# Idle products of the identity with itself ahead of tensor-engine parts in an attention and two-layer feed-forward kernel, with new seeds for its planner

## The chip, the cores and the metric

The kernel runs on one core of one Trainium2 chip. The metric is device time in microseconds (us), the median of several runs. The profile is one further execution, taken by the hardware profiler. Engines: PE is the tensor engine (matrix products, with weight loads beside them as PEld), DVE the vector engine, ACT the scalar engine, POOL the general one, SP the one that only issues transfers (DMAs). PSUM is the memory into which PE writes, SBUF the other on-chip memory.

## The reference, cut to what matters

Windowed attention over chunks of 32 queries (16 keys to the left, 8 to the right and 8 memory keys), then a gated layer (3072 tokens, 512 to 1536 to 512), then a second layer with softmax gating and normalization (512 to 1024 to 512).

```python
scores = scale * np.matmul(q_c, k_full.transpose(0, 1, 3, 2))
a = np.exp(scores - np.max(scores, axis=-1, keepdims=True))
a = a / (np.sum(a, axis=-1, keepdims=True) + 1e-09)
out[:, :, c_start:c_end] = np.matmul(a, v_full)
...
x = (1.0 / (1.0 + np.exp(-(x @ w_gate))) * (x @ w_val)) @ w_out
h = x @ w_in
solu = h * sm
ln = (solu - mu) / np.sqrt(var + 1e-06) * g_ln
return ln @ w_out2
```

## The kernel before, in words

The 3072 tokens are 24 tiles of 128, and 6 blocks of four tiles. Of each tile, attention is a chain of parts that change engines: raw keys `rk` and queries `rq` are loaded (SP, line 472), PE turns them (`d_k`, `d_q`, through `d_turn`, line 456: four transposes against `ident`), ACT and POOL copy them from PSUM to `kT` and `qT`, PE makes the score products (`d_scores`, through `two_banks`, line 515), DVE takes maximum and difference, ACT the exponential, DVE the sums, PE turns the result (`d_p`), ACT copies it to `pT`, PE multiplies with the values `vw` (`d_pv`, line 515), DVE normalizes into the tile `s` (line 597), PE turns it (`d_x`), and ACT and DVE split the turned rows into `xh` and `xl` (lines 610 and 614). The value tiles `vw` are loaded in many small transfers (lines 563 to 570) and completed from a small copy `mv` (line 583).

The weights arrive as raw 64-bit numbers in pieces of 512 KB (line 418). Each piece passes ACT (line 214), three DVE operations (lines 219, 220, 223), ACT (line 279) and POOL (line 230) before PE can use it as `wa`. Two pieces (gate and value) make one of 12 column groups m. `up(j, m, gv)` (line 629) is 12 products of 128x512 for block j into one PSUM buffer `u`; line 635 (ACT) and line 640 (DVE) read it. `down` (line 721), `prod` (line 774) and `out_mm` (line 866) are the later layers.

In PSUM the turned tiles and the `up` results share buffers: tag `u0` (two buffers) holds `d_k`, `d_x` and the memory keys, and `up` with gv 0; tag `u1` (two buffers) holds `d_q`, `d_p`, and `up` with gv 1. A part on PE waits until the buffer that it takes has been read out.

The order of all this is made by `Plan.order`: a list scheduler that knows a fixed duration of each part, its dependencies and its buffers, and takes of the parts that can start the one with the earliest due time. `SHIFTS` is a list of seeds and widths by which all due times are moved at random before it starts. What comes out is one order of instructions for each engine; the engines then run it in that order, each part when its inputs and buffers are there. Planned times are used for nothing else before.

Of the kernel before, what the change touches and what calls it, by code (L numbers as in the profile page):

```python
# [22 lines left out]
class Plan:  # L23
# [5 lines left out]

    HOP, WAIT, ISSUE, DGE, START, LAND, AHEAD, LANES = 0.2, 0.1, 0.48, 0.45, 0.75, 1.95, 40.0, 8  # L30

    SHIFTS = [(2011, 4), (2036, 2), (2116, 1), (2137, 0.5)]

    def __init__(self, caps):
        self.caps, self.tasks = caps, {}
# [98 lines left out]
def encoder_kernel(  # L134
# [313 lines left out]
        make_identity(nc, ident)  # L448


    def d_turn(tag, src):
        rows = src.shape[0]
        ps = pu.tile([128, 512], F32, tag=tag, name="tr")
        pv = ps[:, 0:KM * rows].rearrange("p (k r) -> p k r", k=KM)
        for kk in range(KM):
            nc.tensor.transpose(pv[:, kk, :], src[:, 2 * kk:2 * kk + 2, :], ident[0:rows, 0:rows])  # L456
        return pv
# [48 lines left out]

    def two_banks(lhsT, rhs):
        ps = pa.tile([128, 2, 512], F32, tag="a", name="ps")
        ps = ps[:, :, 0:KM * 64].rearrange("p x (k w) -> p x k w", k=KM)
        for kk in range(KM):  # L510
            for c in range(4):
                o = slice(CH * c, CH * c + CH)
                for x in range(2):
                    r = slice(D * x, D * x + D)
                    nc.tensor.matmul(ps[o, x, kk, :], lhsT=lhsT[r, kk, o], rhs=rhs[r, kk, c, :], start=True, stop=True)  # L515
        return ps
# [102 lines left out]

    def up(j, m, gv, w):  # L620
        u = pu.tile([128, 512], F32, tag=f"u{gv}", name="u")
        u = U[j, m, gv, w] = u[:, 0:w[1] - w[0]]
        xh, xl = X[j]
        n = 0
        for kk in range(KM):
            wh = wa[m][:, gv, 0, kk * 128:(kk + 1) * 128]
            wl = wa[m][:, gv, 1, kk * 128:(kk + 1) * 128]
            for a, c in ((wh, xh), (wh, xl), (wl, xh)):
                nc.tensor.matmul(u, lhsT=a, rhs=c[:, kk, w[0]:w[1]], start=(n == 0), stop=(n == 3 * KM - 1))  # L629
                n += 1  # L630
# [254 lines left out]
    ))  # L885
    add = plan.add
    ACT, DVE, POOL, PE, SP = "act", "dve", "pool", "pe", "sp"
    FIRST, RATE, LEAD, SLACK, EARLY, LATER = 30.0, 1.12, 30.0, 3.0, 140.0, 235.0

    ALONE = "c2", "nt", "gcol", "mhalf", "ident", "zero", "pb"  # L890

    def one(nm, t, eng, dur, fn, deps=(), **kw):
        add((nm, t), eng, dur, lambda: fn(t), deps=[d if isinstance(d, tuple) or d in ALONE else (d, t) for d in deps],
            prev=(nm, t - 1), **kw)
# [17 lines left out]
    for t in range(NTILE):  # L912
        n, u = divmod(t, 2)
        b, i = divmod(t, TB)
        early = t < 2
        one("rk", t, SP, 0.1, lambda t: d_load("rk", t), acq=[("rk", t)], dma=[1.456])
        one("dk", t, PE, 0.9 if early else 0.5, d_k, ["ident", "rk"], acq=[("u0", ("dk", t)), ("kT", t)], rel=[("rk", t)], slack=0 if t < 6 else SLACK)
        one("dkev", t, ACT, 1.35, d_kev, ["dk"], rel=[("u0", ("dk", t))])
        one("dhalo", t, POOL, 0.6, d_halo, ["dkev"] + ([("dhalo", t - 1)] if i else []))
        one("dkmem", t, POOL, 0.45, d_kmem, ["dkev", ("dmev", b)])  # L920
        one("rq", t, SP, 0.1, lambda t: d_load("rq", t), acq=[("rq", t)], dma=[1.456])
        one("dq", t, PE, 0.9 if early else 0.5, d_q, ["ident", "rq"], acq=[("u1", ("dq", t)), ("qT", t)], rel=[("rq", t)], slack=0 if t < 6 else SLACK)
        one("dqev", t, ACT, 0.58, d_qev, ["dq"], rel=[("u1", ("dq", t))])
        one("sw", t, PE, 1.3 if early else 0.75, d_scores,
            ["dqev", "dkmem", ("dhalo", t if i == TB - 1 else t + 1)],
            acq=[("a", t), ("s", t)], rel=[("qT", t), ("kT", t)], slack=0 if t < 6 else SLACK)
        one("max", t, DVE, 1.45, a_max, ["sw"], rel=[("a", t)])
        one("exp", t, ACT, 0.63, a_exp, ["max"], table="exp")
        one("sum", t, DVE, 1.25, a_sum, ["exp"])
        one("dp", t, PE, 0.9 if early else 0.5, d_p, ["exp"], acq=[("u1", ("dp", t)), ("pT", t)], slack=0 if t < 6 else SLACK)  # L930
        one("dpev", t, ACT, 0.58, d_pev, ["dp"], rel=[("u1", ("dp", t))])
        one("pv", t, PE, 1.3 if early else 0.75, d_pv, ["dpev", ("dv", n, 0), ("dv", n, 1), ("dvm", n)],
            acq=[("a", (t, 2))], rel=[("pT", t)] + ([("vw", n)] if u else []), slack=0 if t < 6 else SLACK)
        one("norm", t, DVE, 0.69, d_norm, ["pv", "sum"], rel=[("a", (t, 2))])
        x = [("xh", t // 4), ("xl", t // 4)] if t % 4 == 0 else []
        one("dx", t, PE, 0.9 if early else 0.5, d_x, ["norm"], acq=[("u0", ("dx", t))] + x, rel=[("s", t)], slack=0 if t < 6 else SLACK)
        one("xhi", t, ACT, 0.58, a_xhi, ["dx"] + ([] if t % 4 == 0 else [("xhi", t - 1)]))
        one("xlo", t, DVE, 0.69, a_xlo, ["xhi"], rel=[("u0", ("dx", t))])

# [193 lines left out]
        plan.tasks[n]["due"] = clock  # L1133

    ctx.enter_context(tc.manual_schedule())
    for part in plan.order():
        part["fn"]()


# [31 lines left out]
```

## Time and profile before

| | |
|---|---|
| three runs, median | 954.02 us (951.13 to 954.1) |
| the profiled execution, its own time | 954.97 us |
| its span, first to last instruction | 953.2 us |
| PE busy | 918.1 us, 96% of the span |
| DVE busy | 616.6 us, 65% |
| ACT busy | 425.3 us, 45% |

The profile gives, for any stretch, each engine's busy time, the granted clock of PE, and for a single instruction what ended the idle time before it. A pace on PE is read from the starts of successive instructions, since the ends are modelled and overlap the next start.

### The profile page before, as it was taken

The page shows a single profiled execution, that of the slowest core. Times are in us where ns is not written, and L with a number is a line of the kernel's source. Part 1 is how long each engine was busy: PE and PEld are TensorE (multiplying, and loading weights), DVE is VectorE, ACT ScalarE, POOL GpSimd, SP SyncE. Part 2 cuts the span into 40 slices and gives each one's busy share as a digit, 9 for nine tenths or more (in the row PEclk, how much of TensorE's full clock was granted, in tenths as well). Part 3 has the DMA queues.
Part 4 walks back from the last instruction along what each step waited for, and adds up shares of the span by engine and source line. Part 5 has one row for each costly group of instructions (what it writes and reads, how often), then busy time and mean ns, then how long its engine had stood idle before and what let it go on. Part 6 is the DMA issues. An engine that isn't in the chain of part 4 may idle for free.

```text
span 953.2 us, 17904 instructions
## 1 busy us (share of the span) xinstructions
PE 918.1 (96%) x7144; PEld 596.5 (63%) x7144; DVE 616.6 (65%) x1145; ACT 425.3 (45%) x688; POOL 89.8 (9%) x154
## 2 busy tenths in 40 slices
PE   5599899999999999999999999999999999999998
PEld 4387678878878888888878544444444444444443
DVE  2798684665586666768556356775864863777581
ACT  4458531632454452246335244544634633554462
POOL 1143330000100000000003300000000000000000
PEclk9799899999999999999999999999999999999999
DMA  9989995594478548432773532443244144232324
GB/s 158 243 182 250 203 237 187 153 194 159 118 182 216 155 136 191 155 127 69 244 252 125 174 89 66 100 104 96 67 104 107 55 111 100 75 93 45 78 66 100
DMA packets 201363, 132.64 MB, mean 139 GB/s; under 512 B 152960, under 2 KB 167296, under 8 KB 201088
## 3 DMA queue, kind: packets, MB, share of 16 engines
q1 hardware_dynamic: 191040, 105.29, 45.1%
q10 hardware_dynamic: 10240, 26.22, 8.8%
q8 instruction: 56, 0.92, 0.4%
q14 instruction: 27, 0.22, 0.1%
HBM read 86.38 MB, written 33.03 MB: 125 GB/s over the span
## 4 chain that ended last, share of the span: by engine, by line
PE 88%; DVE 5%; DMA 2%; SPq 2%; issue 1%; ACT 1%; POOL 0%; DVEq 0%; ACTq 0%
PE u L629 37%; PE y L721 20%; PE ps L866 13%; PE Q L774 5%; PE tr L456 4%; PE R L774 3%; PE P L774 3%; PE ps L515 3%; DVE w L220 2%; SPq L570 1%; DVE w L223 1%; DVE w L219 1%; DMA vw<-in_v_dram 1%; DMA rk<-in_k_dram 1%; DMA vw<-mv 1%
## 5 line engine op out<-in xcount | busy, mean ns | idle before, releaser
L629 PE MATMUL u<-xh,wa 128*128 128x512 f32 x1152 | 371.6, 397 | 1.7 <-DVE xl L614 1.0
L629 PEld LDWEIGHTS u<-xh,wa 128*128 128x128 f32 x1152 | 218.3, 190 | 48.7 <-DVE xl L614 1.6
L629 PE MATMUL u<-xl,wa 128*128 128x512 f32 x576 | 226.0, 392 | 0.5 <-DVE xl L614 0.5
L721 PE MATMUL y<-gh,pl 128*128 128x512 f16 x576 | 177.9, 379 | 0.0
L721 PEld LDWEIGHTS <-pl 128*128 128x128 f16 x864 | 84.4, 98 | 102.0 <-DMA pl<-wd 0.3
L866 PE MATMUL ps<-wo,nt 128*128 128x512 f16 x576 | 127.6, 379 | 0.8 <-ACT o L873 0.8
L629 PEld LDWEIGHTS u<-xl,wa 128*128 128x128 f32 x576 | 109.3, 190 | 22.6 <-DVE xl L614 1.0
L721 PE MATMUL y<-gl,pl 128*128 128x512 f16 x288 | 109.2, 379 | 0.0
L640 DVE TENSOR_TENSOR g<-sg,u 128x512 f32<-128x512 f32 x72 | 49.4, 686 | 89.9 <-PE u L629 66.6
L442 ACT ACTIVATE gh<-gi,gm 128x512 f16<-128x512 f32 x72 | 51.7, 720 | 120.2 <-PE y L721 115.7
L232 DVE SCALAR_TENSOR_TENSOR gl<-gi,gm,gh 128x512 f16<-128x512 f32 x72 | 53.6, 749 | 75.4 <-ACT gh L442 75.3
L866 PEld LDWEIGHTS <-nt 128*128 128x128 f16 x576 | 56.4, 98 | 69.0 <-issue 1.3
L635 ACT ACTIVATE sg<-u 128x512 f32<-128x512 f32 x72 | 42.9, 596 | 119.7 <-PE u L629 105.3
L774 PEld LDWEIGHTS <-yh 128*128 128x128 f16 x336 | 32.9, 98 | 39.6
L214 ACT ACTIVATE w<-r 128x512 f32<-128x512 f32 x46 | 30.7, 671 | 50.9 <-DMA wd<-w 10.7
L834 POOL TENSOR_TENSOR ls<-ls,mhalf 128x1 f32<-128x1 f32 x24 | 14.6, 608 | 360.1 <-DVE ls L830 334.1
L774 PE MATMUL Q<-pl,yh 128*128 128x512 f16 x144 | 42.8, 379 | 0.0
L291 DVE TENSOR_REDUCE gm<-g 128x1 f32<-128x512 f32 x60 | 41.0, 685 | 1.8
L220 DVE SCALAR_TENSOR_TENSOR w<-r,w 128x512 int32<-128x512 int32 x46 | 39.8, 865 | 1.6
L219 DVE TENSOR_SCALAR w<-w 128x512 int32<-128x512 int32 x52 | 25.2, 484 | 22.3 <-ACT w L214 22.0
L230 POOL TENSOR_TENSOR wa<-w,wa 128x512 fp32r<-128x512 f32 x24 | 32.6, 1358 | 72.9 <-ACT wa L279 72.9
L795 DVE TENSOR_TENSOR pl<-Q,pl 128x512 f32<-128x512 f32 x36 | 24.7, 687 | 22.7 <-PE Q L774 22.6
(124 smaller groups left out, 1109.4 us busy)
## 6 DMA issues: line engine op xcount, KB each, us to landing
gd<-g SPq DMA_DIRECT2D x72, 256.0 KB
gi<-gd SPq DMA_DIRECT2D x72, 256.0 KB
r<-in_moe_w_out_dram ACTq DMA_DIRECT2D x28, 512.0 KB
vw<-in_v_dram SPq DMA_DIRECT2D x64, 98.0 KB
rk<-in_k_dram SPq DMA_DIRECT2D x24, 256.0 KB
rq<-in_q_dram SPq DMA_DIRECT2D x24, 256.0 KB
out_dram<-o SPq DMA_DIRECT2D x24, 256.0 KB
wd<-r SPq DMA_DIRECT2D x20, 256.0 KB
```

The lines of the kernel that those rows point to most:

```text
L219: nc.vector.tensor_single_scalar(out=d, in_=d, scalar=3, op=ALU.logical_shift_left)
L220: nc.vector.scalar_tensor_tensor(out=d, in0=lo, scalar=29, in1=d, op0=ALU.logical_shift_right, op1=ALU.bitwise_or)
L232: nc.vector.scalar_tensor_tensor(out=dst, in0=x, scalar=s, in1=hi, op0=ALU.mult, op1=ALU.subtract)
L291: nc.vector.tensor_reduce(out=dst, in_=a, axis=AX.X, op=ALU.max, apply_absolute_value=True)
L442: nc.scalar.activation(out=dst, in_=x, func=AF.Copy, scale=s)
L456: nc.tensor.transpose(pv[:, kk, :], src[:, 2 * kk:2 * kk + 2, :], ident[0:rows, 0:rows])
L629: nc.tensor.matmul(u, lhsT=a, rhs=c[:, kk, w[0]:w[1]], start=(n == 0), stop=(n == 3 * KM - 1))
L635: nc.scalar.activation(out=sg, in_=U.pop((j, m, 0, w)), func=AF.Sigmoid)
L640: nc.vector.tensor_tensor(out=g, in0=U.pop((j, m, "s", w)), in1=U.pop((j, m, 1, w)), op=ALU.mult)
L721: nc.tensor.matmul(y, lhsT=a, rhs=c, start=(f == 0 and n == 0), stop=(f == MF - 1 and n == 2))
L774: nc.tensor.matmul(ps, lhsT=yc[a][:, c, kk, u * 128:(u + 1) * 128], rhs=t[:, hl, kk, :], start=(first and n == 0), stop=(n == 5), skip_gro ...
L866: nc.tensor.matmul(ps, lhsT=nt[:, a, kk, :], rhs=C["wo2"][:, c, kk, :], start=(n == 0), stop=(n == 3 * K2 - 1))
```

## The change

Three things are edited. `keep_busy` emits `idle[0]` products of the 128x128 identity with itself, into the PSUM buffer that the part behind them is about to fill; it is called in `d_turn`, `two_banks` and `up`. The number is set where the parts are emitted: for a PE part that the plan starts before 130 us, it is the planned gap ahead of that part less 0.35, divided by 0.45 (before 8 us) or 0.26. The planned durations of the first two tiles' PE parts become those of all other tiles. And `SHIFTS` has other seeds, so that all due times differ, and with them the order on all engines.

```diff
-    SHIFTS = [(2011, 4), (2036, 2), (2116, 1), (2137, 0.5)]
+    SHIFTS = [(1000, 1), (1003, 0.5), (1006, 4), (1009, 0.5), (1024, 4), (1033, 1), (1043, 2), (1068, 2)]
...
+    idle = [0]
+
+    def keep_busy(ps):
+        for _ in range(idle[0]):
+            nc.tensor.matmul(ps[:, 0:128], lhsT=ident, rhs=ident, start=True, stop=True)
+        idle[0] = 0
...
     def d_turn(tag, src):
         rows = src.shape[0]
         ps = pu.tile([128, 512], F32, tag=tag, name="tr")
+        keep_busy(ps)
...
     def two_banks(lhsT, rhs):
         ps = pa.tile([128, 2, 512], F32, tag="a", name="ps")
+        keep_busy(ps[:, 0])
...
     def up(j, m, gv, w):
         u = pu.tile([128, 512], F32, tag=f"u{gv}", name="u")
+        keep_busy(u)
...
+    BUSY = 130.0
...
-        one("dk", t, PE, 0.9 if early else 0.5, d_k, ["ident", "rk"], acq=[("u0", ("dk", t)), ("kT", t)], rel=[("rk", t)], slack=0 if t < 6 else SLACK)
+        one("dk", t, PE, 0.5, d_k, ["ident", "rk"], acq=[("u0", ("dk", t)), ("kT", t)], rel=[("rk", t)], slack=0 if t < 6 else SLACK)
...
+    last = 0.6
     for part in plan.order():
+        if part["eng"] == PE:
+            if part["at"] < BUSY:
+                idle[0] = max(0, int((part["at"] - last - 0.35) / (0.45 if part["at"] < 8 else 0.26)))
+            last = part["end"]
         part["fn"]()
```

The other planned PE durations that change are those of `dq`, `dp` and `dx` (0.9 to 0.5) and of `sw` and `pv` (1.3 to 0.75), for the first two tiles alone.

Eighty-seven such products are emitted in all, 75 ahead of the first `up` and 12 behind it. All orders below are those of PE; `tr` is a turned tile (in: raw keys `rk`, raw queries `rq`, memory keys `mm`, or `s`), `ps` a score product (in: `kT`, `qT`) or a value product (in: `vw`, `pT`), `u` the result of `up`.

PE, from the third tile's scores to the first product of `up`, before:

```order
L515 MATMUL ps<-kT,qT 32x64 x32
L515 MATMUL ps<-vw,pT 32x64 x32
L456 MATMUL tr<-ident,s 128x128 x4
L515 MATMUL ps<-vw,pT 32x64 x32
L456 MATMUL tr<-ident,s 128x128 x8
L515 MATMUL ps<-vw,pT 32x64 x64
L456 MATMUL tr<-ident,s 128x128 x12
L629 MATMUL u<-xh,wa_84 128x512
```

and in the change (from the query tile that the plan now has later):

```order
L455 MATMUL tr<-ident 128x128 x21
L465 MATMUL tr<-ident,rq 128x128 x4
L525 MATMUL ps<-vw,pT 32x64 x32
L465 MATMUL tr<-ident,s 128x128 x4
L525 MATMUL ps<-kT,qT 32x64 x32
L525 MATMUL ps<-vw,pT 32x64 x32
L465 MATMUL tr<-ident,s 128x128 x4
L455 MATMUL ps<-ident 128x128 x7
L525 MATMUL ps<-vw,pT 32x64 x32
L465 MATMUL tr<-ident,s 128x128 x12
L525 MATMUL ps<-vw,pT 32x64 x32
L455 MATMUL tr<-ident 128x128 x13
```

(four transposes of `s`, seven identity products and the first product of `up` follow). The fourth tile's queries are now turned behind 21 identity products; the last two value products no longer stand side by side; 13 and 7 identity products stand ahead of the last transposes and of the first `up`.

PE, from the value product of the fifth tile on, in block 0, before (between products of `up` with `wa_89` and with `wa_1102`):

```order
L456 MATMUL tr<-ident,rk 128x128 x4
L515 MATMUL ps<-vw,pT 32x64 x32
L456 MATMUL tr<-ident,rk 128x128 x4
L456 MATMUL tr<-ident,rq 128x128 x4
L456 MATMUL tr<-ident,s 128x128 x4
L629 MATMUL u<-xh,wa_1102 128x512
```

and in the change (between `up` with `wa_88` and `wa_89`):

```order
L465 MATMUL tr<-ident,s 128x128 x4
L465 MATMUL tr<-ident,rk 128x128 x4
L465 MATMUL tr<-ident,mm 128x32 x4
L455 MATMUL tr<-ident 128x128
L465 MATMUL tr<-ident,rq 128x128 x4
L455 MATMUL tr<-ident 128x128 x6
L465 MATMUL tr<-ident,s 128x128 x4
L525 MATMUL ps<-vw,pT 32x64 x64
L465 MATMUL tr<-ident,rk 128x128 x4
L465 MATMUL tr<-ident,s 128x128 x4
L455 MATMUL tr<-ident 128x128
L465 MATMUL tr<-ident,rq 128x128 x4
```

(four identity products and `up` with `wa_89` follow). Ten attention parts of two tiles now stand in one row without a product of `up` between them, the value products of both tiles side by side, and 12 identity products among them; before, the longest such row has five parts.

PE, in block 1, the longest row of parts before:

```order
L456 MATMUL tr<-ident,s 128x128 x8
L456 MATMUL tr<-ident,rq 128x128 x8
L456 MATMUL tr<-ident,rk 128x128 x4
```

and two of those in the change:

```order
L465 MATMUL tr<-ident,rk 128x128 x4
L465 MATMUL tr<-ident,mm 128x32 x4
L465 MATMUL tr<-ident,rq 128x128 x8
L465 MATMUL tr<-ident,s 128x128 x8
...
L465 MATMUL tr<-ident,s 128x128 x16
L465 MATMUL tr<-ident,rq 128x128 x4
L465 MATMUL tr<-ident,rk 128x128 x4
```

Six parts now stand in one row at three later places (these two and one in block 3); four of the six take buffers of one tag in the first of them.

On SP the fourth tile's queries and, directly behind them, the first raw weight piece (line 418) stood ahead of nine value loads and two loads from `mv`; now the nine value loads come first, then those queries, the two loads from `mv`, and then the weight piece. The first block's `down` parts stood between the last block's `up` parts before, and all stand behind them now.

## Rows read from the trace of the kernel before

**Rows 1.** The page, parts 1 and 3: busy time, and the instruction transfers of PE

```profile
PE 918.1 (96%) x7144; PEld 596.5 (63%) x7144; DVE 616.6 (65%) x1145; ACT 425.3 (45%) x688; POOL 89.8 (9%) x154
...
q8 instruction: 56, 0.92, 0.4%
```

**Rows 2.** Busy time by stage: length, PE, PEld, DVE, ACT, POOL, granted clock, DMA, GB/s

```profile
0.00:50.00 50.00, 28.17 (x593) 21.64 (x594) 25.68 (x49) 21.93 (x48) 9.11 (x25) 0.83 1.01 207
50.00:150.00 100.00, 93.22 (x914) 75.56 (x913) 78.99 (x115) 53.77 (x100) 33.80 (x38) 0.97 0.94 221
150.00:530.00 380.00, 378.13 (x3705) 309.60 (x3704) 243.51 (x464) 154.26 (x256) 29.27 (x63) 1.00 0.59 167
530.00:954.00 424.00, 418.57 (x1938) 189.70 (x1936) 268.47 (x518) 195.32 (x285) 17.57 (x29) 1.00 0.35 87
```

**Rows 3.** Timeline of PE up to the first products of `up`: start, length, instruction, wait

```profile
12.53 1.94 PE L456 MATMUL tr<-ident,rk 128*128 128x128 f32 x8 [2.06 <-DMA rk<-in_k_dram]
...
31.54 0.39 PE L515 MATMUL ps<-vw,pT 64*32 64x64 f32 x2 [5.59 <-DMA vw<-mv]
...
37.66 0.27 PE L515 MATMUL ps<-vw,pT 64*32 64x64 f32 x2 [0.73 <-ACT pT L547]
...
43.60 1.09 PE L456 MATMUL tr<-ident,s 128*128 128x128 f32 x4 [2.36 <-DVE s L597]
45.36 0.79 PE L629 MATMUL u<-xh,wa 128*128 128x512 f32 x1 [0.67 <-ACT xh L610]
46.67 0.79 PE L629 MATMUL u<-xl,wa 128*128 128x512 f32 x1 [0.52 <-DVE xl L614]
...
50.63 0.62 PE L629 MATMUL u<-xh,wa 128*128 128x512 f32 x2
...
53.14 0.39 PE L629 MATMUL u<-xl,wa 128*128 128x512 f32 x1
```

**Rows 4.** Stretches of equal granted clock around both late falls, columns as in rows 2

```profile
36.50:43.10 6.60, 3.44 (x140) 2.53 (x138) 3.98 (x8) 4.55 (x8) 1.37 (x2) 1.00 1.09 316
43.30:50.00 6.70, 5.21 (x13) 3.65 (x14) 6.35 (x11) 3.05 (x5) 2.33 (x2) 0.50 1.09 345
...
91.00:97.80 6.80, 4.08 (x139) 3.31 (x137) 3.21 (x4) 3.60 (x6) 2.43 (x2) 1.00 1.08 287
97.90:104.60 6.70, 5.72 (x18) 4.60 (x19) 2.74 (x5) 3.02 (x4) 1.28 (x1) 0.50 1.12 218
```

**Rows 5.** Timeline of PE from 72 to 105 us

```profile
72.64 0.60 PE L456 MATMUL tr<-ident,rk 128*128 128x128 f32 x4
73.07 0.60 PE L456 MATMUL tr<-ident,rq 128*128 128x128 f32 x4
74.65 0.66 PE L456 MATMUL tr<-ident,rk 128*128 128x128 f32 x4 [0.97 <-ACT sg L635]
...
89.82 0.65 PE L456 MATMUL tr<-ident,s 128*128 128x128 f32 x4 [0.68 <-ACT qT L504]
...
93.60 0.86 PE L515 MATMUL ps<-vw,pT 64*32 64x64 f32 x64
94.26 0.82 PE L515 MATMUL ps<-kT,qT 64*32 64x64 f32 x61
98.88 0.42 PE L515 MATMUL ps<-kT,qT 64*32 64x64 f32 x3 [3.80 <-issue]
...
100.00 0.78 PE L629 MATMUL u<-xh,wa 128*128 128x512 f32 x1
...
104.77 0.40 PE L629 MATMUL u<-xh,wa 128*128 128x512 f32 x1
```

**Rows 6.** Timeline of DVE: one weight piece, lines 219 to 223, and what follows

```profile
43.97 0.59 DVE L219 TENSOR_SCALAR w<-w 128x512 int32<-128x512 int32 x1
...
45.93 0.68 DVE L614 TENSOR_TENSOR xl<-tr,xh 128x512 fp32r<-128x512 f32 x1
```

**Rows 7.** Timeline of PE in block 1's longest row of attention parts

```profile
210.10 0.66 PE L456 MATMUL tr<-ident,rq 128*128 128x128 f32 x4 [0.78 <-ACT qT L504]
```

More of the change, by code (lines that the diff above doesn't have):

```diff
@@ L921, in encoder_kernel @@
         one("rq", t, SP, 0.1, lambda t: d_load("rq", t), acq=[("rq", t)], dma=[1.456])
-        one("dq", t, PE, 0.9 if early else 0.5, d_q, ["ident", "rq"], acq=[("u1", ("dq", t)), ("qT", t)], rel=[("rq", t)], slack=0 if t < 6 else SLACK)
+        one("dq", t, PE, 0.5, d_q, ["ident", "rq"], acq=[("u1", ("dq", t)), ("qT", t)], rel=[("rq", t)], slack=0 if t < 6 else SLACK)
         one("dqev", t, ACT, 0.58, d_qev, ["dq"], rel=[("u1", ("dq", t))])
-        one("sw", t, PE, 1.3 if early else 0.75, d_scores,
+        one("sw", t, PE, 0.75, d_scores,
             ["dqev", "dkmem", ("dhalo", t if i == TB - 1 else t + 1)],
@@ L929, in encoder_kernel @@
         one("sum", t, DVE, 1.25, a_sum, ["exp"])
-        one("dp", t, PE, 0.9 if early else 0.5, d_p, ["exp"], acq=[("u1", ("dp", t)), ("pT", t)], slack=0 if t < 6 else SLACK)
+        one("dp", t, PE, 0.5, d_p, ["exp"], acq=[("u1", ("dp", t)), ("pT", t)], slack=0 if t < 6 else SLACK)
         one("dpev", t, ACT, 0.58, d_pev, ["dp"], rel=[("u1", ("dp", t))])
-        one("pv", t, PE, 1.3 if early else 0.75, d_pv, ["dpev", ("dv", n, 0), ("dv", n, 1), ("dvm", n)],
+        one("pv", t, PE, 0.75, d_pv, ["dpev", ("dv", n, 0), ("dv", n, 1), ("dvm", n)],
             acq=[("a", (t, 2))], rel=[("pT", t)] + ([("vw", n)] if u else []), slack=0 if t < 6 else SLACK)
@@ L935, in encoder_kernel @@
         x = [("xh", t // 4), ("xl", t // 4)] if t % 4 == 0 else []
-        one("dx", t, PE, 0.9 if early else 0.5, d_x, ["norm"], acq=[("u0", ("dx", t))] + x, rel=[("s", t)], slack=0 if t < 6 else SLACK)
+        one("dx", t, PE, 0.5, d_x, ["norm"], acq=[("u0", ("dx", t))] + x, rel=[("s", t)], slack=0 if t < 6 else SLACK)
         one("xhi", t, ACT, 0.58, a_xhi, ["dx"] + ([] if t % 4 == 0 else [("xhi", t - 1)]))
```

## The prediction

> **What bounds the kernel now.** PE does. Its busy time is 918.1 us [rows 1], so about 35 us of the span are left in which it stands still. The stage table [rows 2] says where: 21.8 us of the first 50, 6.8 of the next 100, 1.9 of the 380 behind those, 5.4 of the rest. So what can be won lies before 150 us, where the change puts its products, and what can be lost lies there and in the 380 us that are nearly full. Next come the timelines of the first stretch [rows 3] and of 72 to 105 us [rows 5], and the granted clock around them [rows 4]. Two losses are to be seen. The first products of `up` run at half pace: from 46.67 to 50.63 us ten of them start 0.396 us apart, from 50.63 to 53.14 us eleven start 0.228 us apart [rows 3]; the clock was 0.50 from 43.3 to 50 us, after 6.6 us in which PE was busy for 3.44 [rows 4]. And at 94.26 us a score product stops after 61 of its 64 records for 3.80 us that nothing in the profile explains ("issue"), and the clock falls again behind it [rows 4, 5]. What is missing there is probably the instructions: PE's 14,288 records came in 56 transfers, 255 in each [rows 1], and a value and a score product of 64 records each, with as many loads, stand side by side there from 93.60 us on [rows 5], 256 instructions in under 2 us.
>
> One caution: for the first 15 us the clock is recorded as 1.00, but eight transposes take 1.74 us to the next start (the row's end less 0.2), twice what they take at 72.64 us, four in 0.43 [rows 3, 5]. The durations decide.
>
> **What an identity product costs.** No row has one. A transpose of 128x128 takes 0.107 us at full pace (four in 0.43 [rows 5]). The order prints a score product as 32 instructions where the trace has 61 and 3 records [rows 5], so an f32 product that is no transpose makes two; I estimate 2 x 0.107 = 0.215 us for an identity product, with 0.107 as the lower bound and 0.43 at half clock as the upper. 87 of them are 19 us at full pace; what counts is where they stand.
>
> **Part 1, the first `up`.** Twenty identity products (13 and 7, 4.3 us) stand where PE now waits 2.36, 0.67 and 0.52 us [rows 3]. I expect the clock to be full when `up` begins: ten steps at 0.228 instead of 0.396 us, **-1.7**. Bounds: 0 if the clock falls anyway; -2.8 if the eleven steps from 45.36 to 50.63 us all run freely. The start itself I leave where it is. The value product that waited 5.59 us for its last load [rows 3] may start earlier, as one weight load is moved out of its way, but DVE then begins the weights later and has split three pieces instead of four when `up` starts. A piece is 1.96 us of DVE [rows 6]; this debt is paid in part 3. The 21 products ahead of the fourth tile's queries lie in the wait for a load and cost nothing; the shorter planned durations are only the planner's.
>
> **Part 2, the stop at 94 us.** The value and the score product that stood side by side there are parted now. The stop goes, -3.8, and so does the slow stretch behind it: eleven steps from 100.00 to 104.77 us instead of 2.5, -2.3 [rows 5]. **-6.1**, bounds 0 and -6.1.
>
> **Part 3, ten parts in one row.** Between two products of `up` there now stand ten parts of two tiles, among them the whole way from the turned probabilities to the turned result. That way needs a copy by ACT, a value product, a normalization by DVE, a transpose and two more copies, and nothing of `up` is put between. The nearest rows are the first stretch, where the same way is walked with nothing between: PE waits 0.73 us for `pT`, 2.36 for `s`, 0.67 and 0.52 for `xh` and `xl` [rows 3], 4.3 us for one tile. Two tiles side by side share ACT and DVE, so between 4.3 and 8.6; I take the middle, 6.4. Off it goes what these parts wait for now, 0.97 and 0.68 us [rows 5]: **+4.8** (2.7 to 7.0). The piece that DVE is behind lies in this.
> The 12 identity products inside (2.6 us) are free only where the part behind them waits for its input. Where it waits for its PSUM buffer they wait for the same buffer, and delay it by their own length. PE takes its parts in the order written: the transposes at 74.65 us waited 0.97 us for a buffer, and the product of `up` behind them started only after them [rows 5]. Half of the 2.6 us: **+1.3** (0 to 2.6).
> The Trainium skill, page "TensorE: Matmul & The Clock Gate", section "The mechanism" of its part 3, says that matmuls start and end in program order, none passing another. By that all 12 count wherever a buffer is late, and this term would be 2.6; no row here has an identity product to show it.
> Behind such a row the clock may fall. In the 6.8 us around the stop at 94 us PE was busy for 4.08, and the clock then went to 0.50 [rows 4]; the `up` behind it lost 2.3 us [rows 5]. The ten-part row waits longer, so **+2.3** (0 to 2.3).
>
> **Part 4, the rest of the order.** Three more rows of six parts, where five was the longest. Four parts on one tag have two buffers, so the third and fourth wait for a copy. The row of five parts in block 1 shows one such wait, 0.78 us [rows 7]; two in each, three times, 4.7, less the 1.9 us that PE idles now in this whole stage [rows 2]: **+2.8** (0 to 7.5, if each has four and nothing is taken off). The `down` parts behind the last `up` cost nothing: PE is full there [rows 2]. Some 350 more instructions (four for each identity product) are one or two transfers more, during long products: nothing.
>
> **Sum.** -1.7 - 6.1 + 4.8 + 1.3 + 2.3 + 2.8 = +3.4 us. The sum is made against the profiled execution's own 954.97 us: 958.4. That execution is 0.95 us above the median of the runs shown, so I forecast **957.4 us**. With all terms at their ends it goes from 947.8 to 972.8.
>
> **The rivals.** Faster or slower here means by over 0.3% of 954.02, 2.9 us, about what a measurement of this kernel can tell from none.
> *The waits of the long row overlap (ends faster).* The two tiles' ways run beside each other, so the row waits as long as one tile does, +2.7; the identity products keep the clock up, and the six-part rows cost nothing: -7.8 + 2.7 = -5.1, **948.9**. It decides for faster where all costs of parts 3 and 4 together stay below 4.9 us. For it: 1.9 us of idle time in 380 show how well such waits are hidden now [rows 2]. Against it: they are hidden by `up`, which the long row lacks. Chance 0.18.
> *Costs and gains cancel.* The long row as above, 1.3 for identity products, no fall of the clock, 2.8 for the rest: 6.8 - 7.8 = -1.0, **953.0**. Chance 0.27.
> *The stop moves instead of going.* Two value products stand side by side in the long row, and more such pairs follow. If a transfer of instructions is late at one, part 2 gains nothing: +6.1, **963.5**. Against it: of the present pairs only one stopped. Chance 0.12.
> *The products do not do what they are for.* If they fail to hold the clock ahead of `up`, part 1 gives nothing: **959.1**. The Trainium skill, same page, section "Part 4: PE-mode transpose", says that transposes do not count as activity for the clock; identity products are no transposes, so that page speaks against this rival here. The trace shows transposes at half pace at 12.53 us [rows 3], after a wait as well, so it does not separate the two. Chance 0.08.
>
> **How the numbers follow.** The forecast has 0.35 and, by itself, 955.5 to 960.5. Faster: the first rival, 0.18. Same: the second and 0.02 of the forecast's lower edge, 0.29. Slower: the rest, 0.53. For eight in ten the range leaves out the far part of the first rival and what lies beyond the moved stop: **949.5 to 963.5**.
>
> **What would show it.** Right: the first product of `up` begins near 46 us with starts 0.23 us apart; identity products take about 0.21 us; no wait by "issue" near 94 us; between 73 and 95 us PE waits more than 5 us in a row of ten parts, with ACT or DVE as releaser; the clock reads 0.50 once behind it; PE idles more than 1.9 us between 150 and 530 us. Wrong: that row waits under 3 us and the later stage stays as full as now, which gives the first rival; or PE stops by "issue" again; or `up` starts at 0.40 us a step. A first `up` later than 48 us would mean that the debt of DVE is paid there, and part 1 would be a loss.

## The result, and the profile after

The changed kernel takes **964.5 us** (median of four runs, 962.9 to 966.6) beside 953.4 us of the kernel before on the same chip: a ratio of 1.0117, interval 1.009 to 1.0145. That is 11 us slower. The sign was forecast, the size was not: 957.4 us, with a range that ended at 963.5.

The profiled execution of the change took 966.63 us by its own time, its span is 964.8 us; that is 11.66 us more than the profiled execution before. The page, parts 1 and 3:

```profile
PE 934.4 (97%) x7318; PEld 613.6 (64%) x7318; DVE 611.3 (63%) x1145; ACT 420.5 (44%) x684; POOL 88.5 (9%) x154
...
q8 instruction: 57, 0.93, 0.4%
```

There are 174 records more, two for each identity product as estimated, and one more instruction transfer [rows 1]. Busy time by stage, columns as in [rows 2]:

```profile
0.00:50.00 50.00, 36.93 (x719) 32.82 (x720) 19.27 (x40) 17.75 (x41) 6.40 (x23) 0.93 1.02 206
50.00:150.00 100.00, 94.74 (x940) 78.22 (x939) 81.47 (x123) 58.09 (x102) 34.78 (x38) 0.97 0.91 215
150.00:530.00 380.00, 376.74 (x3703) 309.06 (x3701) 239.84 (x463) 146.67 (x254) 24.14 (x63) 1.00 0.59 168
530.00:965.00 435.00, 425.97 (x1962) 193.52 (x1960) 270.67 (x521) 197.94 (x287) 23.21 (x31) 1.00 0.35 86
```

PE is busier than before in the first two stages, yet it gets less done: identity products and half pace count as busy. In the last stage it stands still for 9.0 us; before, 5.4 [rows 2]. Busy time does not tell where the time went. A better measure is PE's **lag**: the start of a part, less the pure length of all parts ahead of it at full pace (2.72 us for twelve products of `up`, 0.43 for four transposes, 0.72 for a score or value product, 2.59, 1.30 and 5.18 for `down`, `prod` and `out_mm`, all from undisturbed rows). The lag grows by waits, by identity products, by half pace, and by tenths of a us wherever one kind of part follows another, in which PE still counts as busy (before, it grows by 11.7 us between 150 and 530 us, where PE stands still for 1.9). Worked out from the traces:

| lag of PE, us, at | 62 | 106 | 150 | 530 | 630 | 945 us |
|---|---|---|---|---|---|---|
| before | 34.7 | 44.9 | 47.8 | 59.5 | 59.5 | 60.6 |
| the change | 39.0 | 50.6 | 51.8 | 64.9 | 70.6 | 72.3 |
| difference | +4.3 | +5.7 | +4.0 | +5.3 | +11.1 | +11.7 |

Two places stand out: the time up to the first `up`, and something at 612 us, where the forecast saw nothing. Timeline of PE up to the first `up` (beside [rows 3]):

```profile
28.58 0.66 PE L465 MATMUL tr<-ident,rq 128*128 128x128 f32 x4 [1.83 <-DMA rq<-in_q_dram]
...
32.86 0.34 PE L525 MATMUL ps<-vw,pT 64*32 64x64 f32 x7
36.27 1.11 PE L525 MATMUL ps<-vw,pT 64*32 64x64 f32 x56 [3.08 <-issue]
37.32 1.11 PE L465 MATMUL tr<-ident,s 128*128 128x128 f32 x4
38.23 2.44 PE L455 MATMUL ps<-ident 128*128 128x128 f32 x14
40.59 0.76 PE L525 MATMUL ps<-vw,pT 64*32 64x64 f32 x52
43.03 0.33 PE L525 MATMUL ps<-vw,pT 64*32 64x64 f32 x12 [1.67 <-issue]
...
49.63 0.66 PE L465 MATMUL tr<-ident,s 128*128 128x128 f32 x4 [0.57 <-DVE s L607]
50.13 1.73 PE L455 MATMUL u<-ident 128*128 128x128 f32 x14
51.61 0.48 PE L640 MATMUL u<-xh,wa 128*128 128x512 f32 x1
```

PE stops twice by "issue", 4.75 us in all, inside value products, and the first `up` starts at 51.61 instead of 45.36 us. Between the stops lie 56, 4, 14 and 52 records: 126, with as many weight loads 252 instructions. At 50.13 us 14 records (seven identity products) take 1.48 us: **0.21 us** for one.

The clock in stretches of equal granted clock (beside [rows 4]):

```profile
51.60:55.20 3.60, 3.20 (x16) 2.43 (x15) 3.53 (x6) 1.29 (x2) 1.35 (x1) 1.00 0.85 176
87.50:94.30 6.80, 5.23 (x128) 4.90 (x130) 4.19 (x10) 3.53 (x10) 2.61 (x6) 0.50 1.11 272
98.80:101.70 2.90, 2.90 (x16) 2.35 (x15) 2.80 (x5) 1.30 (x2) 0.90 (x2) 1.00 1.12 292
616.60:620.00 3.40, 3.40 (x10) 1.20 (x9) 2.87 (x4) 2.51 (x4) 0.00 (x0) 0.50 0.91 202
```

The first `up` runs at the full 2.4 GHz, as forecast. The fall at 97.8 us and the stop of 3.80 us [rows 4, 5] are gone; the clock is low in the row of ten parts instead, from 87.5 to 94.3 us. The row of ten parts:

```profile
83.48 0.60 PE L465 MATMUL tr<-ident,s 128*128 128x128 f32 x4
...
85.44 0.43 PE L465 MATMUL tr<-ident,mm 32*128 32x32 f32 x4 [0.92 <-ACT sg L646]
86.57 0.49 PE L455 MATMUL tr<-ident 128*128 128x128 f32 x2 [0.70 <-DVE g L651]
...
89.07 2.93 PE L455 MATMUL tr<-ident 128*128 128x128 f32 x12 [1.58 <-ACT pT L557]
91.79 1.06 PE L465 MATMUL tr<-ident,s 128*128 128x128 f32 x4
...
97.89 1.16 PE L455 MATMUL u<-ident 128*128 128x128 f32 x8 [1.49 <-DVE xl L624]
98.81 0.48 PE L640 MATMUL u<-xh,wa 128*128 128x512 f32 x1
```

It lasts 15.3 us for 4.8 us of pure work. The waits in it are 4.7 us together, the 12 identity products last 4.2 us (2.6 at full pace; six of them run at half pace, from 89.07 to 91.79), the rest is mostly half pace.

At 612 us, four engines' timelines:

```profile
597.17 0.59 POOL L845 TENSOR_TENSOR ls<-ls,mhalf 128x1 f32<-128x1 f32 x1 [49.25 <-DVE ls L841]
603.82 0.43 POOL L434 PARTITION_ALL_REDUCE gm<-gm  x1 [6.05 <-issue]
611.79 0.59 POOL L845 TENSOR_TENSOR ls<-ls,mhalf 128x1 f32<-128x1 f32 x1 [7.54 <-issue]
...
612.41 0.15 DVE L849 TENSOR_SCALAR ls<-ls 128x1 f32<-128x1 f32 x1 [6.80 <-POOL ls L845]
...
613.45 1.04 ACT L855 CAST hi<-so 128x1024 f16<-128x1024 f32 x1 [7.43 <-DVE so L850]
...
615.02 2.04 ACT L738 ACTIVATE pl<-y 128x512 f32<-128x512 f32 x4
...
615.65 0.38 PE L732 MATMUL y<-gh,pl 128*128 128x512 f16 x1 [3.92 <-ACT pl L738]
```

Read it from below. PE's first `down` of block 2 waits 3.92 us for ACT, which should have copied block 1 out of PSUM. ACT is stuck in front of that copy with the cast of a normalized tile, which waits for DVE, which waits for POOL. POOL has one all-reduce (the spread of block 3's maxima, `gm`) between the two powers of the first two tiles, and stands still by "issue" for 6.05 us ahead of it and 7.54 us behind it; at both places the trace has MODIFY_POOL_CONFIG records. The Trainium skill, page "GPSIMD Engine Reference", section "2.1 Instruction dispatch", puts what the first call of a freshly loaded POOL kernel pays on top at about 6 us; 6.05 agrees, the 7.54 on the way back is longer. In the kernel before both powers come first, at 593.93 and 595.71 us, then the all-reduce at 603.00 after 6.29 us of "issue", and the next power is due only at 626.16 us, so the same change was paid by nobody. Here it costs PE 3.92 us, and 1.7 us more at half clock: 5.8 us of lag.

### The profile page after: what moved, and what is told of

The parts are those of the page before. It is cut to its first block, busy times and chain, and to the rows that moved or that the text cites. A ratio compares the mean times of both kernels' runs of the same rounds, so it can differ in the third digit from the quotient of the medians.

```text
span 964.8 us, 18248 instructions
## 1 busy us (share of the span) xinstructions
PE 934.4 (97%) x7318; PEld 613.6 (64%) x7318; DVE 611.3 (63%) x1145; ACT 420.5 (44%) x684; POOL 88.5 (9%) x154
## 4 chain that ended last, share of the span: by engine, by line
PE 86%; DVE 4%; issue 3%; ACT 3%; DMA 1%; SPq 1%; POOL 1%; ACTq 0%; POOLq 0%; DVEq 0%
PE u L640 38%; PE y L732 18%; PE ps L877 12%; PE Q L785 5%; PE tr L465 4%; PE ps L525 4%; PE R L785 3%; PE P L785 3%; DVE w L220 1%; PE tr L455 1%; DVE so L827 1%; DMA vw<-mv 1%; SPq L589 1%; DVE w L219 0%; DMA rk<-in_k_dram 0%
## 5 line engine op out<-in xcount | busy, mean ns | idle before, releaser
L220 DVE SCALAR_TENSOR_TENSOR w<-r,w 128x512 int32<-128x512 int32 x46 | 35.7, 776 | 1.6
L223 DVE SCALAR_TENSOR_TENSOR w<-r,w 128x512 int32<-128x512 int32 x46 | 34.8, 757 | 1.6
```

What stands on the lines that cost most here:

```text
L220: nc.vector.scalar_tensor_tensor(out=d, in0=lo, scalar=29, in1=d, op0=ALU.logical_shift_right, op1=ALU.bitwise_or)
```

## The experiments

Two questions: do the identity products cost anything, or is it the order; and what are the stops by "issue"?

**1. The order alone** (no identity product):

```diff
-    BUSY = 130.0
+    BUSY = 0.0
```

> The changed kernel without any identity product: the new seeds and the shorter planned durations alone. Theory (the two stops of 3.1 and 1.7 us ahead of the first product of up come from where the 48 products ahead of them put the transfers' ends): no stop by issue over 1 us before 50 us, the first product of up at 46 to 48 us, but at half clock, 0.40 us a step; the wait at 615 us stays; time 957 to 961. Rival (the new order itself is late before 50 us and loses in the ten-part row): first product of up at 50 us or later, time 962 or more.

Measured: 962.9 us, ratio 1.0112 (1.0083 to 1.0142), the change's own ratio within 0.1%. Timeline of PE:

```profile
29.85 1.11 PE L465 MATMUL tr<-ident,rq 128*128 128x128 f32 x4 [8.60 <-DMA rq<-in_q_dram]
...
40.86 0.68 PE L525 MATMUL ps<-vw,pT 64*32 64x64 f32 x32 [3.96 <-issue]
```

A miss for the theory: a stop of 3.96 us is there without any identity product, and the first `up` starts at 50.75 us, at half clock. **The new order makes the loss, and the products change it by nothing that can be measured.** (The order comes from the seeds and the shorter planned durations together; they were not tried apart.) The fourth tile's queries come late in it (29.85 us; before, the products of that tile's scores could begin at 25.10), and its value and score products then stand close together.

**2. The products alone** (before's seeds and durations, products by the rule of the change, 62 of them):

```diff
+            if part["at"] < 130.0:
+                idle[0] = max(0, int((part["at"] - last - 0.35) / (0.45 if part["at"] < 8 else 0.26)))
```

> The kernel before with its own seeds and durations, and identity products by the same rule as in the change (62, of which 36 ahead of the first value product and 7 behind the first product of up). Theory: the 144 instructions ahead of the first value products put a transfer's end into that dense stretch, as the 128 small ones did: one or two stops by issue, 3 to 6 us together, before 50 us; the first up at full pace but at 48 to 52 us; the stop at 94 us changed; time 951 to 957. Rival (the products are free and hold the clock): first up by 46 us, time 945 to 949.

Measured: 954.6 us, ratio 1.001 (0.9996 to 1.0025): no difference. Stops by "issue" of 1.32, 2.81 and 2.69 us appear at 28, 37.5 and 44 us; the stop at 94 us is gone. The lag is 6.0 us above before's at 62 us, and equal to it from 150 us on (47.7 and 47.8).

**3. and 4. Half a transfer and a whole one** (before's kernel, 32 or 64 small products ahead of the first transposes):

```diff
+            nc.tensor.matmul(ps[0:32, 0:64], lhsT=ident[0:64, 0:32], rhs=ident[0:64, 0:64], start=True, stop=True)
...
+    COUNT = {("dk", 0): 32}
```

> The kernel before with 32 small products (64 deep, 32 by 64, the shape of the value products) ahead of the first transposes, where the tensor engine waits for its first load anyway. They are 128 instructions and change nothing else: every later instruction stands half a transfer of 256 further on. Theory (a stop by issue comes where a whole transfer of 256 instructions is used up faster than the next one arrives): the stop of 3.80 us at 94 us shrinks to about 1 us, the slow stretch behind it goes, and the time falls by 3 to 6 us, to 947.5 to 950.5; a stop under 1 us may appear near 35 us. Rival (the dense pair of products stops for a reason of its own, such as the loads under way at that time): the stop stays at 3.5 to 4 us and the time within 1 us of 953.4.

> As the last, with 64 small products, 256 instructions: a whole transfer further on, so that the transfers' ends fall on the same instructions as before. Theory: the stop at 94 us is back with 3.5 to 4 us and the slow stretch behind it, time within 1 us of 953.4. Rival (any instruction put in ahead moves the stop, or the small products themselves help): the same time as with 32. The other rival (density alone): stop in both.

With 128 instructions more, PE's timeline has no stop behind the pair that stopped before, and two new ones:

```profile
38.76 0.45 PE L524 MATMUL ps<-vw,pT 64*32 64x64 f32 x28 [1.91 <-issue]
...
46.03 0.87 PE L524 MATMUL ps<-vw,pT 64*32 64x64 f32 x37 [4.63 <-issue]
...
101.14 0.85 PE L524 MATMUL ps<-kT,qT 64*32 64x64 f32 x64
```

With 256 it is back, behind the same 61 of 64 records as in [rows 5]:

```profile
102.68 0.81 PE L524 MATMUL ps<-kT,qT 64*32 64x64 f32 x61
106.83 0.30 PE L524 MATMUL ps<-kT,qT 64*32 64x64 f32 x3 [3.34 <-issue]
```

A count over all traces settles the cause of the stops: each of the 19 stops by "issue" of over 1 us (in 13 of the 16 traces) has 193 or 194 of PE's records (products, weight loads, semaphore instructions) more than a multiple of 256 ahead of it. They come at the ends of the transfers of 256 instructions. Times: 955.1 us (1.0029, 1.0009 to 1.005) and 961.9 us (1.0103, 1.0084 to 1.0123). Neither is the forecast: 64 records of a small product took 7.0 us, 0.11 each, and pushed the whole start back; only the places of the stops can be read here.

The transfer itself is in the trace. Of before, DMA between 96.2 and 97.5 us, during the stop:

```profile
q8 instruction: 1, 0.02, 5.8%
```

Of the change, DMA between 33.05 and 34.70, and between 40.25 and 41.45 us:

```profile
q8 instruction: 1, 0.02, 6.0%
...
q8 instruction: 1, 0.02, 5.7%
```

Each time one transfer of 0.02 MB lies in the window, and PE goes on 1.4 to 1.6 us behind its end (98.88, 36.27, 43.03). This fits a transfer that is asked for only when the 256 instructions before it are begun (the pair that stops begins at 93.60 us [rows 5], the transfer 2.6 us later), so that a stretch which uses them up in 1.5 us waits for the rest. The place of a stop is the program's, its size is not: PE's instructions up to 50 us are the same in the change and in runs 6, 8 and 12, and the stops at the same two places come to 4.75, 3.2, 4.0 and 2.0 us. The Trainium skill, page "Runtime: NRT & Kernel Launch", section "Instruction fetch mechanics", has the same blocks of 256 and calls their cost mostly hidden, since the sequencer issues more slowly than they arrive; for these small products it is not so here, with stops of up to 4.6 us.

**5. The kernel before once more:**

> The kernel before, unchanged, profiled once more. If the stop at 94 us belongs to the program (the place of the transfer's end), it is there again behind the same 61 of 64 records, with 3 to 4 us and a slow stretch behind it, whatever the time of this execution is (950 to 956). If it is an accident of one execution, it is smaller than 1 us or at another record, and the part of the forecast that rests on it (6.1 us) was too large against the median.

```profile
98.41 0.42 PE L515 MATMUL ps<-kT,qT 64*32 64x64 f32 x3 [3.79 <-issue]
```

The stop is the program's own, 3.79 us at the same record; 954.7 us in this execution.

**6. The power first** (in the changed kernel):

```diff
+    for name, behind in ((("gmspr", 3), ("lpow", 0, 1)), (("gmset", 3), ("glo", 2, 3))):
+        order.insert(names.index(behind), order.pop(names.index(name)))
```

> The changed kernel with one order swapped: on the general engine the spread of block 3's maxima (the all-reduce) comes behind the power of the second normalized tile, not between the first two, and the vector engine's use of it three parts later. Theory (two changes of the engine's library between two powers, 5.8 and 7.5 us, delay tile two, the copy behind it on ACT, and so the first down part of block 2): the wait of 3.9 us at 615 us and the half clock behind it go, 5 to 6 us, time 958.5 to 959.5. Rival (ACT and DVE are late there for their own load): the wait shrinks by under 2 us, time above 962.

Measured: 959.0 us, ratio 1.0073 (1.005 to 1.0097). POOL's timeline:

```profile
594.28 0.59 POOL L845 TENSOR_TENSOR ls<-ls,mhalf 128x1 f32<-128x1 f32 x1 [50.92 <-DVE ls L841]
601.46 0.56 POOL L845 TENSOR_TENSOR ls<-ls,mhalf 128x1 f32<-128x1 f32 x1 [6.59 <-DVE ls L841]
608.06 0.66 POOL L434 PARTITION_ALL_REDUCE gm<-gm  x1 [6.04 <-issue]
```

POOL waits for DVE ahead of both powers, the standing still ahead of the all-reduce delays nobody, and the wait of 3.92 us is gone: the lag stays at 62.0 us from 530 to 630. The theory holds: the time lies in its range.

**7. Stops moved** (6, and 13 more identity products ahead of the dense stretch):

```diff
+            idle[0] += {("dq", 2): 3, ("dk", 4): 4, ("dq", 3): 6}.get(part["name"], 0)
```

> The changed kernel with the order on the general engine swapped as in the run that put the power first, and 13 more identity products in three waits for loads (3, 4 and 6 ahead of the third tile's queries, the fifth tile's keys and the fourth tile's queries): 52 instructions, so that the transfers of the dense stretch at 30 to 44 us end elsewhere. Theory: both stops there shrink to under 1 us together, the first product of up starts at 46.5 to 48 us, and the time is 3 to 5 us below the 959.0 of that run, 954 to 956. Rival (any place of the ends stops somewhere in 400 instructions without a long wait between them): stops of over 2.5 us stay, time 958 to 961.

Measured: 959.05 us, ratio 1.0063 (1.0044 to 1.0082): the rival. Stops of 1.33 us (39.78) and 1.75 us (46.52) stay, 3.1 us together as in run 6 (0.67 and 2.56). The 278 products from 29.17 to 43.3 us in the change, with their weight loads 556 instructions, hold two transfers' ends wherever the ends fall.

**8. No products in the row of ten** (in the change):

```diff
-    BUSY = 130.0
+    BUSY = 60.0
```

> The changed kernel without the 12 identity products behind the first product of up (the 75 ahead of it stay). Theory of the prediction (half of their 2.6 us delays the row, and they do not keep the clock): 1 to 2 us faster than the change, 962.5 to 963.5, the row of ten parts 1 to 3 us shorter than 15.3. Rival (they stand in waits only): within 0.5 us of 964.5. Other rival (48 fewer instructions move a transfer's end into the value products at 90 us): a stop by issue there, 966 or more.

Measured: 966.8 us, ratio 1.0155 (1.012 to 1.019); not faster. The row is 2 us shorter (82.05 to 95.43). PE's stretch behind it has a granted clock of 0.66 in the mean, so part of it runs at the lower level:

```profile
95.43:99.60 4.17, 4.17 (x13) 3.17 (x14) 3.83 (x6) 2.33 (x5) 2.14 (x2) 0.66 1.00 220
```

The `up` there takes 4.17 us instead of 2.83. The products cost the row 2 us and win back 1.3 by the clock; without them the waits in the row are 5.4 us in place of 4.7. The trace does not show why the median is above the change's; its four runs spread over 8 us.

**9. Twenty products in before's order**, the same 13 and 7 as in the change:

```diff
+    COUNT = {("dx", 3): 13, ("up", 0, 0, 0, (0, 512)): 7}
```

> The kernel before with its own order and only 20 identity products: 13 ahead of the last transposes of s and 7 ahead of the first product of up. Theory: the first product of up still starts at 45 to 46 us, now at full pace (-1.7 us), and the 80 instructions put the transfer's end ahead of the pair of value and score products at 94 us, so that the stop falls from 3.8 to 1 us or less and the slow stretch behind it goes (-5): 945 to 948 against a before of 951.5 to 953.4. Rival (the stop only moves to another pair): a stop of over 2 us by issue elsewhere, time within 2 us of before.

Measured: 951.3 us, ratio **0.9985 (0.9974 to 0.9996)**: a gain, but not the forecast one. No stop by "issue" is left before 150 us. But:

```profile
43.18 3.17 PE L455 MATMUL tr<-ident 128*128 128x128 f32 x26 [1.00 <-DVE xl L623]
46.19 0.60 PE L464 MATMUL tr<-ident,s 128*128 128x128 f32 x4
...
48.11 0.48 PE L639 MATMUL u<-xh,wa 128*128 128x512 f32 x1
```

The products wait for the PSUM buffer of the part that follows, and put it off by their own length: 46.19 instead of 43.60 us. So the full clock behind them wins nothing (lag at 62 us 34.8, before 34.7). In the traces the missing stop and the pace behind it are worth 5.8 us by 106 us, and 3.8 at the end: 1.7 of it goes in one wait of `up` for ACT at 118.32 us.

**10. A buffer of their own** (13 products into a turn of tag `u1`):

```diff
+            ps = pu.tile([128, 512], F32, tag="u1", name="own")
...
+    COUNT = {("dx", 3): 10, ("up", 0, 0, 0, (0, 512)): 3}
```

> The kernel before with its own order and 13 identity products in a PSUM buffer of their own turn (tag u1, free by then) in place of the buffer of the part that follows: 10 ahead of the last transposes of s, 3 ahead of the first product of up. Theory (in the run with twenty the products began only at 43.18 us, when the buffer that they shared came free, and put off the transposes by 2.6 us): they now run in the wait of 2.4 us that is there anyway, the first product of up starts at 45 to 46 us and at full pace (-1.7), no stop by issue over 1 us near 94 us and no slow stretch behind it (-6): 7 to 8 us below before, 944 to 947. Rival (52 instructions in place of 80 leave the stop or bring another; or the buffer was not what held them): first up at 47.5 us or later, or a stop of over 1.5 us; 949 or more.

Measured: 952.2 us, ratio 0.9997 (0.9983 to 1.0012). The products now start at 41.07 us, as the theory says, but a stop by "issue" falls among them:

```profile
44.75 0.49 PE L457 MATMUL own<-ident 128*128 128x128 f32 x2 [1.50 <-issue]
```

The first `up` starts at 46.35 us at full pace, 1.2 us of lag are won by 62 us and 4.1 by the end of the trace; the medians show none of it. Twelve executions range from 950.4 to 955.4 us, those of before from 950.2 to 955.5, and a trace tells of one.

**11. The old start** (6 without products; all parts up to the first `up` in the order of before):

```diff
+    FIRST_PARTS = [
...
+    order = [plan.tasks[n] for n in FIRST_PARTS] + [p for p in order if p["name"] not in set(FIRST_PARTS)]
```

> The changed kernel with the power first and without identity products, all engines' parts up to the first product of up in the order of the kernel before; behind it the order of the change. Theory (the new order costs 4 to 5 us ahead of the first up, by the stops in its dense value and score products and by the later load of the fourth tile's queries, and nothing gives that back): no stop by issue over 1 us before 50 us, first up at 45 to 46 us at half pace, time 952 to 956. Rival (what the old start gains is paid later, in the ten-part row or in waits of up for weights that the vector engine has not split): time 957 or more.

Measured: 957.6 us, ratio 1.0045 (1.0028 to 1.0062). The first `up` starts at 44.87 us, and the lag at 62 us is 34.7, as before. At 106 us it is 48.1, against 48.5 in run 6: **most of what the start wins is paid in the row of ten**, where 13.4 us of lag are added from 62 us on (11.2 in run 6), by waits for ACT (2.56 and 1.83 us) and DVE (2.79). Run 6 has identity products and this run none; beside run 1, which has none either, 5.1 us are won at 62 us, and 1.5 of them are left at 106 and at 150. The rival holds.

**12. The row cut to eight parts** (6, with the ninth tile's keys and the eighth tile's queries behind the `up`):

```diff
+        (UP, ("dx", 4)), (("dk", 8), UP), (("dq", 7), ("dk", 8)), (("dkev", 8), ("whi", 14)), (("dhalo", 8), ("wlo", 14)),
```

> The changed kernel with the power first, and the row of ten parts cut to eight: the transposes of the ninth tile's keys and the eighth tile's queries (with their copies on ACT and POOL) stand behind the product of up that followed the row, so that this product no longer waits for a buffer that they hold; the 4 identity products ahead of it are left out. Theory (what the change loses near 90 us is the row itself): from the end of the product of up ahead of the row to the start of the one behind it 12 us or less in place of 14.8, and 2 to 3 us of it stay to the end: 956 to 957.5. Rival (the row waits for the vector engine's sums and splits, which come no sooner): the product starts under 1 us sooner, 958.5 or more.

Measured: 958.65 us, ratio 1.0064 (1.0042 to 1.0085). The row is 11.2 us long instead of 14.8, and the lag is 1.5 us lower from 150 us (48.2) to the end of the trace, but the median does not move by more than its interval.

**13. and 14. Start and row undone** (as run 11, with all parts up to the `up` that before starts at 106 us in before's order), without products and with the twenty of run 9:

```diff
+    FIRST_PARTS = [
...
+            idle[0] = {("dx", 3): 13, ("up", 0, 0, 0, (0, 512)): 7}.get(part["name"], 0)
```

> The changed kernel with the power first and no identity product, all engines' parts up to the product of up that the kernel before starts at 106 us in the order of that kernel, behind it the order of the change. Only the row of ten parts and the start are undone. Theory A (the row is what the new order costs ahead of 530 us: it takes some 10 us where the old order there takes 2 without its stop and 8 with it): the stop at 94 us is back, 3.5 to 4 us at the same score product, and the time is that of before plus 1 to 2 us, 953 to 955.5. Theory B (the weights come no sooner, and what the old order wins by 106 us is paid behind it): waits of up for the vector engine or ACT of over 2 us together between 106 and 150 us, and 957 or more, as with the old start alone.

> The same with the 13 and 7 identity products of the run with twenty. Theory A: no stop by issue over 1 us near 94 us, first up at full pace, 2 to 4 us less than the run without them: 950.5 to 953. Theory B: no gain from the missing stop, since the vector engine sets the pace by 106 us: within 1 us of the run without them.

Measured: 958.6 us, ratio 1.0073 (1.0045 to 1.01), and 954.6 us, ratio 1.0016 (1.0001 to 1.003). Timeline of PE without the products:

```profile
97.56 0.30 PE L525 MATMUL ps<-kT,qT 64*32 64x64 f32 x3 [2.35 <-issue]
...
109.86 1.07 PE L525 MATMUL ps<-vw,pT 64*32 64x64 f32 x64 [1.37 <-ACT pT L557]
116.58 0.50 PE L640 MATMUL u<-xh,wa 128*128 128x512 f32 x1 [2.27 <-DVE g L651]
```

At 106 us the lag is 41.1, 3.8 below before; at 150 it is 47.8, the same. The waits for ACT and DVE behind 106 us have taken it: theory B in the run without products. The run with them does not fit either theory cleanly: 4 us faster in the median, 1.7 in the trace.

## Why the prediction was right and wrong

**Part 1, the pace:** right. The first `up` runs at full clock, 0.23 us a step, and an identity product costs 0.21 us. With the rule that the forecast cited from the Trainium skill (page "TensorE: Matmul & The Clock Gate", section "Part 4: PE-mode transpose": transposes do not count as activity for the clock) the traces agree: in run 1 transposes in a row from 12.29 to 15.87 us stay at half pace (0.86 us for four), with identity products among them in the change they run at full pace (0.44) from 5.59 us on. Here the starts were read, since the granted clock stands at 1.00 in both.

**Part 1, the start:** here the forecast failed. Its step was "The start itself I leave where it is"; it came 6.25 us later, 4.3 us of lag after the better pace (2.4 to 2.8 in the traces of runs 6, 8 and 12, where the same start has smaller stops). It is the forecast's third rival, a stop that moves, at another place than it named: ahead of the first `up`, where the new order puts a score product between two value products within 4 us. I had compared the pairs near 94 us with instruction transfers and did not do so in the stretch that the orders in the part on the change showed. "Some 350 more instructions ... during long products: nothing" has the same fault: 75 of the 87 products stand ahead of the first `up`, where products are short. That the rival's time, 963.5, lies near the measured one is luck: it let part 2 gain nothing, and part 2 gained. The forecast's test, "a first `up` later than 48 us would mean that the debt of DVE is paid there", is not borne out either: PE waits 0.57 us for DVE ahead of the first `up` and 0.40 in its first step, and 4.75 us in the stops; the late queries are the other difference that the trace shows.

**Part 2:** right, -6.1 in the trace, and its cause (instructions) is shown by runs 3 and 4 and the count behind them. But a removed stop does not reach the end whole: 5.8 at 106 us became 3.8 in run 9.

**Part 3:** right in sum, wrong in its terms, so the sum is luck. Gross cost of the row 10.5 us, forecast 10.0: waits 4.7 (6.4), identity products 4.2 (1.3), the rest mostly half pace inside the row (2.3, behind it). The products' term was too small: they last 2.6 us at full pace and 1.6 more by half pace, and taking them out makes the row 2.0 us shorter (run 8), between the forecast's 1.3 and its upper bound of 2.6. They take the buffer of the part behind them and are done in program order; run 9 shows apart from all else that 13 of them then delay that part by 2.6 us. By the rule of program order that the forecast cited from the Trainium skill (page "TensorE: Matmul & The Clock Gate", section "The mechanism") the term would have been 2.6; that agrees with run 9, and is 0.6 more than run 8 shows for the row.

**Part 4:** 1.3 us between 150 and 530 us, forecast 2.8. The second step that failed is "The `down` parts behind the last `up` cost nothing: PE is full there". It looked at PE alone. The new order also put an all-reduce between two powers on POOL, an engine that is busy 9% of the time, and that cost 5.8 us of lag: half of the whole loss. Run 6 takes it out; by its median 5.5 us, by the ratios (1.0117 and 1.0073) 4.

**The sum** of what the lag shows: 4.3 - 0.3 + 1.3 + 5.8 + 0.6 = 11.7 us, the difference of the two executions. But these are places, not causes that could each be removed: the POOL order can (run 6), the start and the row only in small part (runs 11 to 13: 1.5 us of lag each, not clear in the medians), since PE then waits for DVE and ACT at the next place. What in the new order keeps them behind between 62 and 150 us stays open, and so does the rest of the loss: run 13 has the lag of before at 150 us, and its trace ends 2.4 us above it. The rival in which the products fail to hold the clock fell by the pace of the first `up`. The two that forecast no loss fell too: the row did not get cheaper by overlap, and neither had the start or POOL in it. One slip in the sum: the upper ends of all terms add up to 19.4 us, which gives 973.4 and not 972.8; nothing else was worked out from it.

No version here is faster than before by more than 0.3%. The best is run 9, by 0.15%.

## What to carry to other kernels

A list scheduler with new seeds moves every queue: compare the order on all engines, the idle ones first, and look for operations of a kind that does not stand beside its neighbour without a pause, as an all-reduce between elementwise operations on POOL. Count instructions in stretches of many small products, and treat any instruction put ahead of them as a move of the transfers' ends. Fill idle time with products into a buffer that is free, not into that of the next part.

## What was not expected of the hardware

- A change from an elementwise operation to an all-reduce on POOL and back: 6.05 and 7.54 us of standing still, without a wait that the trace names.
- A stop for instructions of up to 4.6 us, with PE going on 1.4 to 1.6 us behind the transfer's end.
- A product of 64 deep, 32 by 64 took 0.11 us a record when 64 of them, all into one place, stood alone (run 3, 7.0 us in all), while 64 records of a score product of that shape take 1.1 us in all in the same trace (13.66 to 14.77 us, at half pace). What makes the difference was not tried.
- Executions of one kernel differ by 5 us (950.2 to 955.5 in 21 of before). The two traces of it, of executions of 954.97 and 954.68 us, agree within 0.5 us of lag at each place up to the end; none of its faster executions was traced, so where the difference arises stays open, and every lag here is compared with the longer ones.
